# Where the decay mask and the decay powers of a fused attention and two MLPs are made, and in which order its first loads go

## The chip, the cores and the metric

The kernel runs on one core of a Trainium2 chip. The metric is the device time of one execution in microseconds (us); lower is better. One execution of the kernel before was also recorded by the hardware profiler, and every row below is from that record.

## The reference

A linear attention with a decay per head (2 batches, 8 heads, 768 positions, head dimension 64), then two MLPs over its 1,536 tokens (512 to 2048 to 512 channels), all in float32.

```python
rel = pos[:, None] - pos[None, :]
Dmask = np.where(rel >= 0, lam[:, None, None] ** rel, 0.0)
lam_pow = lam[:, None, None] ** (pos[None, :, None] + 1)
for b in range(nb):                       # blocks along the sequence
    intra = (q_b @ k_b.T * Dmask) @ v_b
    inter = (q_b * lam_pow) @ kv_state
    out_b = intra + inter
    kv_state = lam ** block * kv_state + (k_b * lam ** (block - 1 - pos)).T @ v_b
h = x @ w_in;  x = (h * tanh(softplus(h))) @ w_out
h = x @ w2_in; x = (relu(h) ** 2) @ w2_out
```

`lam` holds one number for each of the 8 heads.

## The kernel before

The sequences are cut into 12 chunks of 128 positions (6 for each batch), all heads together. A chunk c takes two loads of 512 KB, `qk{c}` (L379) and `kv{c}` (L381), and these steps, by the names that the plan gives them: `sc{c}` 16 score matmuls on TensorE (L392); `a{c}` the scores times the mask on VectorE, 128x1024; `kd{c}` keys times the last column of the mask on GpSimd (L398); `qd{c}` queries times the powers `pw` on GpSimd (L403); `sd{c}` the update of the state on TensorE (L415); `sa{c}` its addition on VectorE; `ss{c}` the decay of the state (L447 or L451); `xo{c}` the output on TensorE (L433, L437). Each result is split into a high and a low part, `xh` on ScalarE and `xl` on VectorE, since every MLP product is made of three matmuls of such parts (`mm3`, L278).

The MLP weights come as 64-bit numbers in 512 KB loads, `st{L}{g}{kind}{kk}{i}` (L502); each gives one `m` (ScalarE, L507) and one `t` (VectorE, L510), two loads together two bit operations on VectorE (L515), then `wh` (ScalarE) and `wl` (VectorE). The first MLP product, `up` of tokens 0 to 511, needs the first four weight loads (`st00000`, `st00001`, `st00010`, `st00011`) and the outputs of chunks 0 to 3. It is cut in eight groups of six matmuls; the first four need the first pair of weight loads and the first half of the channels alone.

Nothing is scheduled on the chip: the class `Plan` simulates the engines at build time, with a cost and a lag written at every `op`, and the instructions of each engine are emitted in the order that it finds. TensorE takes the ready operation of lowest rank; the other engines the one with the earliest due time. `plan.run(14.0, UNITS)` gives the time from which TensorE's work is counted when due times are worked out. The names in `FIRST` are loads (and steps of SyncE) whose order is written by hand; every other load follows the last of them. Near the end `plan.follow` holds `sc5` and `sd4` behind the third group of the first `up`. SyncE issues all large loads, one after the other; a DMA that waits there holds those behind it.

Mask and powers go through DRAM: ScalarE issues a load of `lam` onto 8 partitions; seven doubling multiplications on VectorE (`powers`, L324) make a table of 8x256 (zeros, a one, the powers); SyncE stores it to `tab_d` (L338), then reads it back with shifted addresses, 128 partitions by 4 heads by 128, in two DMAs for `mask` (L344) and two for `pw` (L351). The pieces of these four DMAs are 512 bytes each: 1,024 for the mask and 512 for the powers. TensorE starts with ten matmuls on zeros (`warm`).

Of the kernel before, what the change touches and what calls it, by code (L numbers as in the profile page):

```python
# [12 lines left out]
F32 = mybir.dt.float32  # L13
# [4 lines left out]
ALU = mybir.AluOpType  # L18
PSUM = bass.MemoryType.PSUM

P = 128
H = 8
D = 64
NP = H // 2
CH = 128
# [6 lines left out]
UNITS = 50  # L32
# [184 lines left out]
def attention_mlps(ctx, tc, lam, qk, kv, w_in, w_out, w2_in, w2_out, out):  # L217
# [7 lines left out]
    nc = tc.nc  # L225
# [9 lines left out]

    units = ctx.enter_context(tc.tile_pool(name="units", bufs=1))
    banks = ctx.enter_context(tc.tile_pool(name="banks", bufs=1, space=PSUM))
    dram = ctx.enter_context(tc.tile_pool(name="dram", bufs=1, space=bass.MemoryType.DRAM))


    FIRST = {n: 0.01 * i for i, n in enumerate(
        "st00000 qk0 tab_d kv0 st00001 masks decays qk1 kv1 qk2 kv2 qk3 kv3 st00010 st00011".split())}

    plan = Plan({"DVE": AHEAD, "ACT": AHEAD, "POOL": AHEAD, "SP": AHEAD})
    op = plan.op

    def tl(v, *shape):

        if v.tile is None:
            if v.space == "P":  # L250
                v.tile = banks.tile([P, 2, TB], F32, tag=f"b{v.slot}", name=v.name)
            else:
                v.tile = units.tile([P, 2 * TB], v.dtype, tag=f"u{v.slot}", name=v.name)
        t = v.tile
        if v.space == "P":
            if not shape:
                return t
            t = t.rearrange("p a b -> p (a b)")
        if not shape:
            shape = (2, TB)  # L260
        if len(shape) == 2:
            return t.rearrange("p (a b) -> p a b", a=shape[0])
        if len(shape) == 3:
            return t.rearrange("p (a b c) -> p a b c", a=shape[0], b=shape[1])
        return t.rearrange("p (a b c d) -> p a b c d", a=shape[0], b=shape[1], c=shape[2])
# [23 lines left out]

    W = 2 * CH
    tab_d = dram.tile([H, W], F32, name="tab_d")
    misc = Val("misc")
    mask = Val("mask")

    def pw():
        return tl(misc, 2, 4, CH)[:, 0]

    def tab():  # L300
        return tl(misc, 4, W)[0:H, 2]

    def warm_up():

# [3 lines left out]

    warm = Val("warm", "P")
    zval = Val("zero", dtype=BF16)  # L310
    misc_parts = [(misc, "pw"), (misc, "tab")]

    def zeros():
        if zval.tile is None:
# [3 lines left out]
    op("DVE", 0.4, lambda: nc.vector.memset(zeros(), 0.0), [], [(zval, 0)], name="zero", due=-9.0)  # L318
    op("PE", 4.3, warm_up, [(zval, 0)], [(warm, 0)], name="warm", rank=-3000)

    def powers():
        t, o, n = tab(), CH - 1, 1
        while n < CH:
            nc.vector.tensor_scalar(  # L324
                out=t[:, o + n + 1 : o + 2 * n + 1], in0=t[:, o + 1 : o + n + 1],
                scalar1=t[:, o + n : o + n + 1], scalar2=None, op0=ALU.mult,
            )
            n *= 2

    def ones():  # L330
        nc.vector.memset(tab()[:, 0 : CH - 1], 0.0)
        nc.vector.memset(tab()[:, CH - 1 : CH], 1.0)

    op("ACT", 0.1, lambda: nc.scalar.dma_start(out=tab()[:, CH : CH + 1], in_=lam), [], [(misc, "lam")],
       name="lam", lag=2.2, due=0.0)
    op("DVE", 0.4, ones, [], [(misc, "tab")], name="ones")
    op("DVE", 1.2, powers, [(misc, "lam")], [(misc, "tab")], name="powers")
    op("SP", 0.1, lambda: nc.sync.dma_start(out=tab_d, in_=tab()), [(misc, "tab")], [("tab_d", 0)],  # L338
       name="tab_d", lag=2.2, due=FIRST["tab_d"])

    def masks():
        for e in range(2):

            nc.sync.dma_start(  # L344
                out=tl(mask, 2, NP, CH)[:, e],
                in_=bass.AP(tab_d.tensor, tab_d.offset + e * W, [[1, P], [2 * W, NP], [1, CH]]),
            )

    def decays():
        for e in range(2):  # L350
            nc.sync.dma_start(  # L351
                out=pw()[e * D : (e + 1) * D],
                in_=bass.AP(tab_d.tensor, tab_d.offset + e * W + CH, [[0, D], [2 * W, NP], [1, CH]]),
            )

    op("SP", 1.6, masks, [("tab_d", 0)], [(mask, 0)], name="masks", due=FIRST["masks"])
    op("SP", 0.9, decays, [("tab_d", 0)], [(misc, "pw")], name="decays", due=FIRST["decays"])


    x_hi, x_lo, x_raw = {}, {}, {}  # L360
# [7 lines left out]
    def attention(j):  # L368
        cs = (2 * j, 2 * j + 1)
        t, i = divmod(j, CPB // 2)  # L370
        s, first, last = 2 * j // SEQ, 2 * j % SEQ == 0, 2 * j % SEQ == SEQ - 2
        rank = -2000 + 50 * j
        qks, kvs, avs, qds = [], [], [], []
        for c in cs:
            q, k, a = Val(f"qk{c}"), Val(f"kv{c}"), Val(f"a{c}")
# [7 lines left out]
        for n, c in enumerate(cs):  # L383
            q, k, a = qks[n], kvs[n], avs[n]
            sc = Val(f"sc{c}", "P")

            def scores(sc=sc, q=q):
                t, o = tl(q, 2, NP, CH), tl(sc, 2, NP, CH)
                for p in range(NP):
                    for e in range(2):  # L390
                        r = slice(e * D, (e + 1) * D)
                        nc.tensor.matmul(out=o[:, e, p], lhsT=t[r, 1, p], rhs=t[r, 0, p], start=True, stop=True)  # L392

            op("PE", 0.95, scores, [(q, "q"), (q, "k")], [(sc, 0)], name=sc.name, rank=rank + n)
            op("DVE", 1.3, lambda a=a, sc=sc: tt(tl(a, 2, NP, CH), tl(sc, 2, NP, CH), tl(mask, 2, NP, CH), ALU.mult),
               [(sc, 0), (mask, 0)], [(a, 0)], name=a.name)
            if not (last and n):
                op("POOL", 1.3, lambda k=k: nc.gpsimd.tensor_tensor(  # L398
                    out=tl(k, NP, 4, D)[:, :, 1:3], in0=tl(k, NP, 4, D)[:, :, 1:3],
                    in1=tl(mask, 2, NP, CH)[:, :, :, CH - 1 : CH].rearrange("p e n o -> p n e o").to_broadcast(  # L400
                        [P, NP, 2, D]), op=ALU.mult), [(k, "k"), (mask, 0)], [(k, "k")], name=f"kd{c}")
            if not first or n:
                op("POOL", 1.35, lambda q=q: nc.gpsimd.tensor_tensor(  # L403
                    out=tl(q, 2, NP, CH)[:, 0], in0=tl(q, 2, NP, CH)[:, 0], in1=pw(), op=ALU.mult),
                   [(q, "q"), (misc, "pw")], [(q, "q")], name=f"qd{c}")
        sd, xo = Val(f"sd{j}", "P"), Val(f"xo{j}", "P")
        for n, c in enumerate(cs):
            if last and n:
# [13 lines left out]
        sv = state[s]  # L422
        for n, c in enumerate(cs):
            fresh = first and n == 0

            def outs(k=kvs[n], a=avs[n], q=qks[n], n=n, fresh=fresh, sv=sv):
                v, w, qd = tl(k, NP, 4, D), tl(a, 2, NP, CH), tl(q, 2, NP, CH)[:, 0]

                z, o = tl(sv, 2, NP, P)[:, n], tl(xo, NP, 2, CH)
                for p in range(NP):  # L430
                    for e in range(2):

                        nc.tensor.matmul(out=o[e * D : (e + 1) * D, p, n], lhsT=v[:, p, 0 if e else 3],  # L433
                                         rhs=w[:, e, p], start=True, stop=fresh)
                    for e in range(0 if fresh else 2):
                        r = slice(e * D, (e + 1) * D)
                        nc.tensor.matmul(out=o[r, p, n], lhsT=z[:, p, r], rhs=qd[:, p], start=False, stop=True)  # L437

            op("PE", 0.95 if fresh else 1.9, outs,
               [(kvs[n], "v"), (avs[n], 0)] + ([] if fresh else [(qks[n], "q"), (sv, n)]),  # L440
               [(xo, n)], name=f"xo{c}", rank=rank + 20 + n)
            if last and n:
                continue
            def scale(sv=sv, n=n):
                z, last = tl(sv, 2, NP, P), pw()[:, :, CH - 1 : CH]
                if t:
                    nc.gpsimd.tensor_tensor(  # L447
                        out=z[:, 1 - n], in0=z[:, n], in1=last.to_broadcast([P, NP, P]), op=ALU.mult)
                    return
                for p in range(NP):  # L450
                    nc.scalar.activation(out=z[:, 1 - n, p], in_=z[:, n, p], func=AF.Copy, scale=last[:, p])  # L451

            if not fresh:
                op("POOL" if t else "ACT", 1.3 if t else 1.2, scale, [(sv, n), (misc, "pw")], [(sv, 1 - n)],
                   name=f"ss{c}")

            def add(sv=sv, n=n, fresh=fresh):
                z, d = tl(sv, 2, NP, P)[:, 1 - n], tl(sd, 2, 2, NP, D)[:, 0, n]
                for e in range(2):
                    r = slice(e * D, (e + 1) * D)  # L460
                    if fresh:
                        nc.vector.tensor_copy(out=z[r, :, r], in_=d[r])
                    else:
                        tt(z[r, :, r], d[r], z[r, :, r], ALU.add)

            op("DVE", 0.9, add, [(sd, n), (sv, 1 - n)], [(sv, 1 - n)], name=f"sa{c}")
# [367 lines left out]
    for o in plan.ops:  # L834
        if o.eng == "SP" and o not in ordered:
            plan.follow(ordered[-1], o)
    order = plan.run(14.0, UNITS)
    if DEBUG:
        DEBUG(plan)
    with tc.manual_schedule():  # L840
# [42 lines left out]
```

## Time and profile before

| | us |
|---|---|
| median of 3 runs | 567.02 (566.72 to 567.08) |
| span of the profiled execution, first to last instruction | 564.7 |
| TensorE matmuls busy, whole span | 549.6 (97%) |
| VectorE busy | 307.6 (54%) |
| ScalarE busy | 333.2 (59%) |
| GpSimd busy | 33.1 (6%) |

The span is 2.3 us shorter than the median; the rest lies around the first and the last instruction. The shares are means over 565 us: they say nothing of the first 35 us, in which TensorE is the least busy.

### The profile page before, as it was taken

To read this page: it belongs to the slowest core of one execution; us is meant where nothing else is said; L and a number is where in the kernel's file an instruction comes from. 1 tells how busy PE (TensorE), PEld (TensorE's weight loads), DVE (VectorE), ACT (ScalarE), POOL (GpSimd) and SP (SyncE) were. 2 spreads that over 40 slices of the span, in tenths; PEclk is the share of its full clock that TensorE was granted. 3 is DMA by queue.
4 is the path that set the end of the run, shared out by engine and by line. 5 is a ranking of instruction groups with operands and counts; after the bars stand their busy time and mean duration, and the time that the engine had idled before them with its cause. 6 is when DMAs were issued, how large, how long until landed. Compare 5 with 4: busy or idle time off the path is not lost.

```text
span 564.7 us, 7047 instructions
## 1 busy us (share of the span) xinstructions
PE 549.6 (97%) x2934; PEld 454.9 (81%) x2934; DVE 307.6 (54%) x339; ACT 333.2 (59%) x374; POOL 33.1 (6%) x31
## 2 busy tenths in 40 slices
PE   3989999999999999999999999999999999999997
PEld 1878888888888888888888888888888888888885
DVE  2876985951453833582688865434363635743301
ACT  1435364643764566545886877347964789546920
POOL 1654600000000000000000000000000000000000
PEclk9899999999999999999999999999999999999999
DMA  8999000222141106041400401311222112300022
GB/s 238 409 409 339 6 2 0 75 74 74 38 149 38 38 2 203 21 122 65 149 1 0 150 0 38 111 39 37 76 74 75 60 48 79 113 0 1 18 95 111
DMA packets 15998, 50.52 MB, mean 89 GB/s; under 512 B 1624, under 2 KB 3168, under 8 KB 15968
## 3 DMA queue, kind: packets, MB, share of 16 engines
q1 hardware_dynamic: 15952, 50.08, 25.5%
q8 instruction: 23, 0.38, 0.3%
q14 instruction: 7, 0.06, 0.0%
q10 hardware_dynamic: 16, 0.00, 0.0%
HBM read 46.92 MB, written 3.15 MB: 89 GB/s over the span
## 4 chain that ended last, share of the span: by engine, by line
PE 96%; DMA 2%; DVE 1%; issue 0%; SPq 0%; DVEq 0%
PE dn L278 46%; PE up L278 20%; PE p L278 13%; PE e L278 7%; PE b L278 3%; PE xo L433 2%; PE sc L392 2%; PE xo L437 1%; DMA mask<-tab_d 1%; PE sd L415 1%; DVE t L510 0%; DMA tab_d<-misc 0%; DVE state L271 0%; DVE misc L324 0%; DMA misc<-in_lam_dram 0%
## 5 line engine op out<-in xcount | busy, mean ns | idle before, releaser
L515 DVE SCALAR_TENSOR_TENSOR t<-m,t 128x1024 int32<-128x1024 int32 x64 | 78.5, 1231 | 63.5 <-ACT m L507 61.4
L268 ACT ACTIVATE ac<-dn 128x1024 f32<-128x1024 f32 x46 | 47.3, 1029 | 101.9 <-PE dn L278 101.9
L271 DVE TENSOR_TENSOR gl<-h,gh 128x1024 fp32r<-128x1024 f32 x48 | 58.7, 1227 | 78.0 <-ACT gh L268 77.6
L278 PE MATMUL dn<-gh,wl 128*128 128x512 f32 x192 | 74.7, 389 | 0.0
L278 PE MATMUL dn<-wh,gh 128*128 128x512 f32 x192 | 74.7, 389 | 0.0
L278 PE MATMUL dn<-wh,gl 128*128 128x512 f32 x192 | 74.7, 389 | 0.0
L278 PE MATMUL dn<-gh,wh 128*128 128x512 f32 x192 | 74.7, 389 | 0.0
L278 PE MATMUL dn<-wl,gh 128*128 128x512 f32 x192 | 74.7, 389 | 0.0
L278 PE MATMUL dn<-gl,wh 128*128 128x512 f32 x192 | 74.7, 389 | 0.0
L268 ACT ACTIVATE gh<-h 128x1024 fp32r<-128x1024 f32 x48 | 50.3, 1053 | 0.7
L507 ACT ACTIVATE m<-st 128x512 f32<-128x512 f32 x64 | 40.1, 664 | 10.5 <-DMA st<-in_moe_w_in_dram 6.8
L271 DVE TENSOR_TENSOR wl<-t,wh 128x1024 fp32r<-128x1024 f32 x32 | 39.6, 1246 | 12.1 <-ACT wh L268 12.1
L606 ACT ACTIVATE h<-up 128x1024 f32<-128x1024 f32 x20 | 20.6, 1029 | 38.2 <-PE up L278 32.5
L268 ACT ACTIVATE wh<-t 128x1024 fp32r<-128x1024 f32 x32 | 33.4, 1052 | 15.3 <-DVE t L515 15.2
L278 PEld LDWEIGHTS dn<-gh,wl 128*128 128x128 f32 x192 | 36.0, 188 | 7.5
L278 PEld LDWEIGHTS dn<-wh,gh 128*128 128x128 f32 x192 | 36.0, 188 | 7.5
L278 PEld LDWEIGHTS dn<-gl,wh 128*128 128x128 f32 x192 | 36.0, 188 | 7.5
L278 PEld LDWEIGHTS dn<-wl,gh 128*128 128x128 f32 x192 | 36.0, 188 | 7.5
L278 PEld LDWEIGHTS dn<-wh,gl 128*128 128x128 f32 x192 | 36.0, 188 | 7.4
L278 PEld LDWEIGHTS dn<-gh,wh 128*128 128x128 f32 x192 | 36.0, 188 | 7.4
L268 ACT ACTIVATE dn<-ac 128x1024 f32<-128x1024 f32 x34 | 34.4, 1019 | 0.2
L510 DVE TENSOR_SCALAR t<-st 128x512 int32<-128x512 int32 x64 | 26.8, 446 | 7.0 <-DMA st<-in_moe_w_in_dram 5.7
(102 smaller groups left out, 987.3 us busy)
## 6 DMA issues: line engine op xcount, KB each, us to landing
st<-in_moe_w_in_dram SPq DMA_DIRECT2D x32, 512.0 KB, 4.7
st<-in_moe_w_out_dram SPq DMA_DIRECT2D x32, 512.0 KB, 3.6
qk<-in_qk_dram SPq DMA_DIRECT2D x12, 512.0 KB, 10.6
kv<-in_kv_dram SPq DMA_DIRECT2D x12, 512.0 KB, 10.4
out_dram<-ac SPq DMA_DIRECT2D x4, 512.0 KB, 2.8
out_dram<-ac SPq DMA_DIRECT2D x4, 256.0 KB, 2.0
mask<-tab_d SPq DMA_DIRECT2D x2, 256.0 KB, 6.3
misc<-tab_d SPq DMA_DIRECT2D x2, 128.0 KB, 6.8
```

The costliest lines, as they stand in the source:

```text
L268: nc.scalar.activation(out=o, in_=i, func=AF.Copy)
L271: nc.vector.tensor_tensor(out=o, in0=a, in1=b, op=alu)
L278: nc.tensor.matmul(out=out_, lhsT=a, rhs=b, start=first and i == 0 and not onto, stop=last and i == 2, skip_group_check=onto)
L392: nc.tensor.matmul(out=o[:, e, p], lhsT=t[r, 1, p], rhs=t[r, 0, p], start=True, stop=True)
L415: nc.tensor.matmul(out=o[e * D : (e + 1) * D, p], lhsT=t[:, p, 1 + e], rhs=t[:, p, 0 if e else 3], start=True, stop=True)
L433: nc.tensor.matmul(out=o[e * D : (e + 1) * D, p, n], lhsT=v[:, p, 0 if e else 3], rhs=w[:, e, p], start=True, stop=fresh)
L437: nc.tensor.matmul(out=o[r, p, n], lhsT=z[:, p, r], rhs=qd[:, p], start=False, stop=True)
L507: op("ACT", 0.67, lambda st=st, i=i: nc.scalar.activation(out=tl(m)[:, i], in_=tl(st, TB, 2)[:, :, 1].bitcast(F32), func=AF.Copy, scale=RA ...
L510: op("DVE", 0.5, lambda st=st, i=i: nc.vector.tensor_scalar(out=tl(t)[:, i], in0=tl(st, TB, 2)[:, :, 0], scalar1=29, scalar2=None, op0=ALU ...
L515: nc.vector.scalar_tensor_tensor(out=tl(t), in0=tl(m).bitcast(I32), scalar=scalar, in1=tl(t), op0=shift, op1=ALU.bitwise_or)
L606: op("ACT", 1.05, lambda: nc.scalar.activation(out=tl(h), in_=tl(src), func=AF.Relu if L else AF.Mish), halves(src), [(h, 0)], name=h.name)
```

## The change

The table in DRAM goes away with its store and its four reads. ScalarE loads `lam` repeated on all 128 partitions (`rate`, 8 values each), and twice more, onto 64 partitions each, every second value of it (`pair_rate`, 4 values). GpSimd writes a 128x128 diagonal of ones. VectorE makes each head's mask as one scan along 128 columns: `state = lam * state + eye`, which is 0 left of the diagonal, 1 on it, then the powers. Eight such scans make the mask (two operations of four, `mask0` and `mask1`), four scans with a start of 1 and nothing added make `pw`. SyncE now issues `qk0 kv0 qk1 kv1` first, then the first two weight loads, then chunks 2 and 3 and the next two weight loads as before. The due times are worked out from 6.0 instead of 14.0.

```diff
     FIRST = {n: 0.01 * i for i, n in enumerate(
-        "st00000 qk0 tab_d kv0 st00001 masks decays qk1 kv1 qk2 kv2 qk3 kv3 st00010 st00011".split())}
+        "qk0 kv0 qk1 kv1 st00000 st00001 qk2 kv2 qk3 kv3 st00010 st00011".split())}
...
-    op("ACT", 0.1, lambda: nc.scalar.dma_start(out=tab()[:, CH : CH + 1], in_=lam), [], [(misc, "lam")],
-       name="lam", lag=2.2, due=0.0)
-    op("DVE", 0.4, ones, [], [(misc, "tab")], name="ones")
-    op("DVE", 1.2, powers, [(misc, "lam")], [(misc, "tab")], name="powers")
-    op("SP", 0.1, lambda: nc.sync.dma_start(out=tab_d, in_=tab()), [(misc, "tab")], [("tab_d", 0)],
-       name="tab_d", lag=2.2, due=FIRST["tab_d"])
...
+    def diagonal():
+        nc.gpsimd.memset(tl(misc, 2, 4, CH)[:, 1, 0:2], 0.0)
+        nc.gpsimd.affine_select(out=eye(), in_=eye(), pattern=[[1, CH]], compare_op=ALU.not_equal, fill=1.0,
+                                base=1 - CH, channel_multiplier=1)
+
+    def rates():
+        nc.scalar.dma_start(out=rate(), in_=bass.AP(lam.tensor, lam.offset, [[0, P], [1, H]]))
         for e in range(2):
...
+            nc.scalar.dma_start(out=pair_rate()[e * D : (e + 1) * D],
+                                in_=bass.AP(lam.tensor, lam.offset + e, [[0, D], [2, NP]]))
+
+    op("ACT", 0.3, rates, [], [(misc, "lam")], name="lam", lag=2.2, due=-9.0)
+    op("POOL", 0.9, diagonal, [], [(misc, "eye")], name="eye", due=-9.0)
+
+    def run_of_powers(out_, lam_, add, first):
+        nc.vector.tensor_tensor_scan(out=out_, data0=lam_.to_broadcast([P, CH]), data1=add, initial=first,
+                                     op0=ALU.mult, op1=ALU.add)
+
+    def masks(n):
+        for h in range(4 * n, 4 * n + 4):
+            run_of_powers(tl(mask, 2, NP, CH)[:, h % 2, h // 2], rate()[:, h : h + 1], eye(), 0.0)
...
     def decays():
...
-    op("SP", 1.6, masks, [("tab_d", 0)], [(mask, 0)], name="masks", due=FIRST["masks"])
-    op("SP", 0.9, decays, [("tab_d", 0)], [(misc, "pw")], name="decays", due=FIRST["decays"])
+        for p in range(NP):
+            run_of_powers(pw()[:, p], pair_rate()[:, p : p + 1], none(), 1.0)
+
+    for n in range(2):
+        op("DVE", 1.3, lambda n=n: masks(n), [(misc, "lam"), (misc, "eye")], [(mask, n)], name=f"mask{n}", due=-8.0 + n)
+    op("DVE", 1.3, decays, [(misc, "lam"), (misc, "eye")], [(misc, "pw")], name="decay", due=2.0)
...
-    order = plan.run(14.0, UNITS)
+    order = plan.run(6.0, UNITS)
```

## Rows read from the trace of the kernel before

**Rows 1.** TensorE's waits, whole span: who waited for whom, us in total, times, longest.
```profile
PE xo L433 <- DVE a L271: 6.8, 1, 6.8
PE sc L392 <- DMA qk<-in_qk_dram: 2.6, 2, 1.3
```

**Rows 2.** Four stretches: length, busy us by engine, granted clock, DMA share, GB/s.
```profile
0.00:13.03 13.03, 5.12 (x26) 2.26 (x26) 2.81 (x13) 2.62 (x3) 1.16 (x5) 0.94 0.84 236
...
14.31:18.84 4.53, 4.53 (x48) 3.91 (x49) 2.80 (x3) 1.06 (x1) 2.21 (x3) 0.57 1.03 410
18.84:32.45 13.61, 11.67 (x213) 10.62 (x209) 12.69 (x18) 7.16 (x18) 7.84 (x7) 1.00 1.03 409
32.45:560.90 528.45, 528.18 (x2652) 438.11 (x2652) 287.36 (x306) 322.39 (x352) 20.62 (x16) 1.00 0.22 75
```

**Rows 3.** The chain that ended last, first 20 us: start, us, what.
```profile
0.73 1.38 DMA misc<-in_lam_dram
...
3.92 1.78 DMA tab_d<-misc
...
6.15 6.75 DMA mask<-tab_d
...
13.03 1.23 DVE a L271
...
16.28 2.01 PE sc L392 x16
...
18.91 1.09 PE sc L392 x16
```

**Rows 4.** Instructions in order of time, first 8 us: start, us, engine, line, operation.
```profile
0.73 0.58 ACTq L334 DMA_DIRECT2D misc<-in_lam_dram  x1
...
1.19 3.96 PE L307 MATMUL warm<-zero 128*128 128x512 bf16 x10 [1.19 <-DVE zero L318]
...
5.11 0.67 ACT L507 ACTIVATE m<-st 128x512 f32<-128x512 f32 x1 [2.48 <-DMA st<-in_moe_w_in_dram]
...
5.11 0.43 DVE L510 TENSOR_SCALAR t<-st 128x512 int32<-128x512 int32 x1 [1.22 <-DMA st<-in_moe_w_in_dram]
...
6.37 1.16 PE L392 MATMUL sc<-qk 64*128 64x128 f32 x16 [1.22 <-DMA qk<-in_qk_dram]
6.70 1.43 SPq L351 DMA_DIRECT2D misc<-tab_d  x2
```

**Rows 5.** Busy time and DMA in one stretch of 1 us, columns as in Rows 2.
```profile
8.00:9.00 1.00, 0.00 (x0) 0.00 (x0) 0.00 (x0) 0.00 (x0) 0.00 (x0) 1.00 1.01 195
```

**Rows 6.** VectorE's groups from 12.9 to 32.5 us: count, busy us, mean ns, idle before.
```profile
L271 DVE TENSOR_TENSOR a<-sc,mask 128x1024 f32<-128x1024 f32 x4 | 4.9, 1222 | 4.3 <-DMA mask<-tab_d 2.5 <-PE sc L392 1.7
L515 DVE SCALAR_TENSOR_TENSOR t<-m,t 128x1024 int32<-128x1024 int32 x3 | 3.7, 1222 | 0.1
L271 DVE TENSOR_TENSOR state<-sd,state 64x256 f32<-64x256 f32 x6 | 2.5, 422 | 0.6 <-PE sd L415 0.4
L510 DVE TENSOR_SCALAR t<-st 128x512 int32<-128x512 int32 x2 | 2.3, 1202 | 0.0
L271 DVE TENSOR_TENSOR xl<-xo,xh 128x512 fp32r<-128x512 f32 x3 | 2.1, 688 | 0.1
L271 DVE TENSOR_TENSOR wl<-t,wh 128x1024 fp32r<-128x1024 f32 x1 | 1.4, 1369 | 0.0
L462 DVE COPY state<-sd 64x256 f32<-64x256 f32 x2 | 0.8, 416 | 0.0
```

**Rows 7.** Instructions in order of time where the first up begins.
```profile
31.13 1.16 PE L392 MATMUL sc<-qk 64*128 64x128 f32 x16 [1.33 <-DMA qk<-in_qk_dram]
...
32.45 0.47 PE L278 MATMUL up<-xh,wh 128*128 128x512 f32 x1 [0.16 <-DVE state L271]
```

**Rows 8.** VectorE, in order of time: a late input of the second token block's up.
```profile
63.65 1.23 DVE L271 TENSOR_TENSOR fl<-xr,fh 128x1024 fp32r<-128x1024 f32 x1
```

**Rows 9.** The chain that ended last: start, us, what, for that up's first matmuls.
```profile
66.34 2.95 PE up L278 x12
```

More of the change, by code (lines that the diff above doesn't have):

```diff
@@ L237, in attention_mlps @@
     banks = ctx.enter_context(tc.tile_pool(name="banks", bufs=1, space=PSUM))
-    dram = ctx.enter_context(tc.tile_pool(name="dram", bufs=1, space=bass.MemoryType.DRAM))
     FIRST = {n: 0.01 * i for i, n in enumerate(
-        "st00000 qk0 tab_d kv0 st00001 masks decays qk1 kv1 qk2 kv2 qk3 kv3 st00010 st00011".split())}
+        "qk0 kv0 qk1 kv1 st00000 st00001 qk2 kv2 qk3 kv3 st00010 st00011".split())}
     plan = Plan({"DVE": AHEAD, "ACT": AHEAD, "POOL": AHEAD, "SP": AHEAD})
@@ L288, in halves @@
         return [(v, 0), (v, 1)]
-    W = 2 * CH
-    tab_d = dram.tile([H, W], F32, name="tab_d")
     misc = Val("misc")
@@ L298, in pw, with eye, none, rate @@
         return tl(misc, 2, 4, CH)[:, 0]
-    def tab():
-        return tl(misc, 4, W)[0:H, 2]
+    def eye():
+        return tl(misc, 8, CH)[:, 4]
+    def none():
+        return tl(misc, 8, CH)[:, 5]
+    def rate():
+        return tl(misc, 8, CH)[:, 6, 0:H]
+    def pair_rate():
+        return tl(misc, 8, CH)[:, 7, 0:NP]
     def warm_up():
@@ L310, in attention_mlps @@
     zval = Val("zero", dtype=BF16)
-    misc_parts = [(misc, "pw"), (misc, "tab")]
     def zeros():
@@ L319, in attention_mlps @@
     op("PE", 4.3, warm_up, [(zval, 0)], [(warm, 0)], name="warm", rank=-3000)
[L321 to L332, printed above, removed]
@@ L334, in attention_mlps @@
-    op("ACT", 0.1, lambda: nc.scalar.dma_start(out=tab()[:, CH : CH + 1], in_=lam), [], [(misc, "lam")],
-       name="lam", lag=2.2, due=0.0)
-    op("DVE", 0.4, ones, [], [(misc, "tab")], name="ones")
-    op("DVE", 1.2, powers, [(misc, "lam")], [(misc, "tab")], name="powers")
-    op("SP", 0.1, lambda: nc.sync.dma_start(out=tab_d, in_=tab()), [(misc, "tab")], [("tab_d", 0)],
-       name="tab_d", lag=2.2, due=FIRST["tab_d"])
-    def masks():
-        for e in range(2):
[L344 to L347, printed above, removed]
@@ L349, in decays @@
-    def decays():
[L350 to L354, printed above, removed]
-    op("SP", 1.6, masks, [("tab_d", 0)], [(mask, 0)], name="masks", due=FIRST["masks"])
-    op("SP", 0.9, decays, [("tab_d", 0)], [(misc, "pw")], name="decays", due=FIRST["decays"])
+    def diagonal():
+        nc.gpsimd.memset(tl(misc, 2, 4, CH)[:, 1, 0:2], 0.0)
+        nc.gpsimd.affine_select(out=eye(), in_=eye(), pattern=[[1, CH]], compare_op=ALU.not_equal, fill=1.0,
+                                base=1 - CH, channel_multiplier=1)
@@ L360, in attention_mlps @@
+    masked = [(mask, 0), (mask, 1)]
+    decayed = [(misc, "pw")]
     x_hi, x_lo, x_raw = {}, {}, {}
@@ L395, in attention @@
             op("DVE", 1.3, lambda a=a, sc=sc: tt(tl(a, 2, NP, CH), tl(sc, 2, NP, CH), tl(mask, 2, NP, CH), ALU.mult),
-               [(sc, 0), (mask, 0)], [(a, 0)], name=a.name)
+               [(sc, 0), *masked], [(a, 0)], name=a.name)
             if not (last and n):
@@ L400, in attention @@
                     in1=tl(mask, 2, NP, CH)[:, :, :, CH - 1 : CH].rearrange("p e n o -> p n e o").to_broadcast(
-                        [P, NP, 2, D]), op=ALU.mult), [(k, "k"), (mask, 0)], [(k, "k")], name=f"kd{c}")
+                        [P, NP, 2, D]), op=ALU.mult), [(k, "k"), *masked], [(k, "k")], name=f"kd{c}")
             if not first or n:
@@ L404, in attention @@
                     out=tl(q, 2, NP, CH)[:, 0], in0=tl(q, 2, NP, CH)[:, 0], in1=pw(), op=ALU.mult),
-                   [(q, "q"), (misc, "pw")], [(q, "q")], name=f"qd{c}")
+                   [(q, "q"), *decayed], [(q, "q")], name=f"qd{c}")
         sd, xo = Val(f"sd{j}", "P"), Val(f"xo{j}", "P")
@@ L453, in attention @@
             if not fresh:
-                op("POOL" if t else "ACT", 1.3 if t else 1.2, scale, [(sv, n), (misc, "pw")], [(sv, 1 - n)],
+                op("POOL" if t else "ACT", 1.3 if t else 1.2, scale, [(sv, n), *decayed], [(sv, 1 - n)],
                    name=f"ss{c}")
```

## The prediction

> **What bounds the kernel now.** I read the stretches first [rows 2]. From 32.45 us on, TensorE is busy 528.18 of 528.45 us: no other engine and no DMA can give back more than 0.27 us there. Whatever the change is worth is therefore decided before the first `up` product, and the question is only how much earlier TensorE can reach that point with the same work done. The waits of TensorE [rows 1] say where it loses time: one wait of 6.8 us of the first `xo` for the first masked scores, and 2.6 us in two waits of score matmuls for `qk` loads. The chain [rows 3] tells what stands behind the long one: `lam` lands at 2.11, the table is stored by 5.70, the mask lands at 12.90 and the first `a` begins at 13.03. After the pause TensorE's clock is also low: in 14.31 to 18.84 the granted clock is 0.57 of full, a mixture of the levels 1.2 and 2.4 GHz [rows 2], after an idle stretch that began when the first scores ended at 7.5 [rows 4]. The same 16 score matmuls take 2.01 us there and 1.09 later [rows 3].
>
> The last thing to see is that three resources are close together between 13 and 32 us. DMA moves 409 to 410 GB/s with a share of 1.03 [rows 2], so it is full; VectorE is busy 12.69 of 13.61 us and TensorE 11.67. The removal of the mask's wait is therefore not worth what the wait was; it is worth the smallest of three leads.
>
> **The change part by part.**
>
> *Removed.* The table's path: from the landing of `lam` at 2.11 to the first `a` at 13.03 [rows 3]. SyncE loses five DMA issues, two of which take 1.43 us together [rows 4], and the wait for the table that held `kv0` and everything behind it. 1,536 pieces of 512 bytes leave the DMA queues. In 8 to 9 us the DMA engines are full at 195 GB/s [rows 5] against 409, which is at most 381 such pieces in a microsecond.
>
> *Added, ScalarE.* Three DMA issues in place of one, 0.58 us each by the one there is [rows 4], so until about 2.5. ScalarE's next useful work waits for a weight load that will land after 10, so the issue time is hidden; if it weren't, it would cost 1.2 us. The loads have 128 pieces of 32 bytes and 512 of 4 bytes. At the rate of the small pieces above, 640 pieces are 1.7 us of all DMA engines; zero if they slip between the large ones. I take 0.5 us off the large loads. `rate` should land like `lam`, at 2.1 to 3.4; the last `pair_rate` at 3.4 (issued at about 2.0, plus 1.38) to some 6.
>
> The Trainium skill (DMA: Bandwidth & Descriptors, Queues, rings and completion order) says that each DMA engine takes turns between the queues that have work, so ScalarE's small loads would not have to wait behind all of SyncE's large ones. The landing of `lam` at 2.11 with a 512 KB load already issued agrees but tests it little, as that load had hardly begun to move.
>
> *Added, GpSimd.* A memset of 256 columns and a select of 128, before anything else that matters; its memset of 1024 columns of state moves behind them. No row shows a select; GpSimd has nothing to do until the mask is there, so I count nothing, and 1 us if the diagonal comes after `rate`.
>
> *Added, VectorE.* Twelve scans of 128 elements. No row shows a scan. Two-source operations take 422 ns for 256 and 1222 for 1024 elements [rows 6], that is 1.04 ns an element and 0.155 fixed, so 0.29 us for 128 as a lower end. Each step of a scan needs the one before it, so it may go slower for each element; I take the row of twice the length, 0.42, and 0.9, about twice that again, as the upper end, since no row excludes it. Twelve are 5.0 us (3.5 to 10.8): from about 2.4, masks are ready at 5.8, powers at 7.5, and the first `a` begins at some 7.7. The powers stand ahead of `a` since the plan finds them ready first.
>
> The Trainium skill (DVE: opcode table, instruction layouts, handler registers and perf-mode slots, Datapath and trigger behaviour) says that the built-in scan runs at half throughput. By that a scan of 128 would cost what 256 elements cost otherwise, an estimate that equals the row I chose; without it the twelve would be 3.5 us and `a` 1.5 us earlier. No run here shows it yet.
>
> *Moved.* `qk0 kv0 qk1 kv1` before the weights, and no table in between. The first load landed at 5.1, the second at 6.37 [rows 4]; a load is 0.524 MB, or 1.28 us at 409 GB/s. So load n lands at 5.1 + 1.28 (n - 1), plus the 0.5: `qk1` near 8, the two weight loads near 11 and 12, `kv3` near 17, the next weights by 19.7, the 17th load at 26.1. The first scores follow the warm-up, which ends at 5.15 [rows 4], about 1.2 earlier than before.
>
> *The sum: when can `up` begin?*
> - TensorE: the work between is 1.16 + 4.53 + 11.67 = 17.4 us [rows 2, 4], less 1.9 if the clock stays at 2.4 GHz (0.92 on the scores, as much again on the `xo` before them). From 5.15 that is 20.6 at the earliest.
> - VectorE: the groups of 12.9 to 32.5 sum to 17.7 us [rows 6], plus 0.9 for two `t` of the first weights, 0.43 each [rows 4], that used to fall into the pause. From 7.7: 26.3 without any idle time. 3.5 us of it (two `t` of 1.2 each and the third bit operation) belong to weights that only the second half of `up` reads: 22.8 if the new order puts them later. With 1 to 2 us of waiting for loads: 24 to 27.5.
> - DMA: six score blocks stand before `up`, and `sc5` is held behind its third group, so the sixth is `sc6`, which waits for the 17th load [rows 7]. If the plan keeps that order, `up` begins at 26.1 + 1.1 = 27.2, 5.2 us earlier than 32.45. If `up` goes first, it begins with VectorE at about 25.5, and `sc6`'s 1.1 us comes later: 32.45 - 25.5 - 1.1 = 5.9.
>
> Both orders give much the same, and I take 5.6 us. The wait of 6.8 and the slow clock's 1.9 would have given 8.7; the difference goes to loads and to VectorE. Of the rest of the span I take the 0.27 of idle time and the 3.8 us after the last matmul as they are. Span 564.7 - 5.6 = 559.1; with the 2.3 us around it 561.4.
>
> **The rivals.**
>
> *A (less gain): the small loads or the scans hold the first `a`.* For it: 512 four-byte pieces on a queue beside full loads, and no row of a scan. Each microsecond that the powers come later moves VectorE's 26.3 by as much. With the powers' `lam` at 6 and 0.6 us a scan, `a` begins near 9.7 and the lead is 2 to 4: 563 to 565. Against it: VectorE can put off 3.5 us.
>
> *B (more gain): the order puts the second weights off.* `up` begins at about 23 with the clock high all along, lead 7 to 8.5, 558.5 to 560. Against it: loads land only at their rate, and the planned order had those operations ahead before.
>
> *C (no change): the lead is given back later.* All orders after 32.45 are planned anew, with due times 8 us earlier. The last `fl` for `up` of the next tokens ends at 64.88 and its matmuls begin at 66.34 [rows 8, 9]: 1.5 us to spare. If VectorE, with 5 us of scans more, comes there no earlier than now, TensorE waits until then and keeps 1.5 at most: 565.5 to 567. Against it: its inputs come earlier too, and over the whole stretch it is busy 287.36 of 528.45 us [rows 2], though that row doesn't say how much of the idle time lies before 65.
>
> *D (slower): scans beyond 0.9 us.* `a` begins later than 13.03 as soon as twelve scans take more than 13.03 - 2.4 = 10.6 us, 0.89 each. At 1.2 us each it is 16.8, 3.8 us later than now, and VectorE's other work is stacked behind, while the earlier `qk` loads can't help: about 570. For it: nothing shows a scan, and a broadcast operand. Against it: of VectorE's groups with 512 or fewer elements [rows 6] only the two `t` take that long, the others 0.69 or less.
>
> **How the numbers follow.** Forecast (lead 4.2 to 7): 0.60, 560 to 562.8. A 0.16, B 0.11, C 0.07, D 0.06. The range reaches into A and B: 558.6 to 564.6. About 0.2% (1.1 us) is what a measurement of this kernel can tell from no change. Faster by more: forecast, A and B, 0.87; within it: most of C, 0.07; slower: D, 0.06.
>
> **What would show it.** `a` first at 7 to 9; scans at 0.3 to 0.5 us; no wait of `xo` above 3 us, and a granted clock near 1.0 from 9 us on; `up` first at 24 to 27.5; DMA at about 410 GB/s from 4 us on; idle time of TensorE after `up` under 1 us. The prediction is wrong if scans or small loads are far from these, or if TensorE gets a new wait between 33 and 80 us.

## The result, and the profile after

The changed kernel takes 569.16 us (median of 5 runs, 568.97 to 571.12), the kernel before 566.72 beside it (566.05 to 567.08): a ratio of 1.0051, 95% interval 1.0034 to 1.0069. It is slower by half a per cent, where 561.4 us was forecast. The profiled execution, 571.12, is the slowest of the five; its span is 569.3 us. Its rows show where the time lies; of how much, the medians (2.4 us) say more than the spans (4.6).

TensorE's waits in the changed kernel: who waited for whom, us in total, times, longest [rows 1].

```profile
PE xo L432 <- DVE a L270: 4.5, 2, 3.6
PE sc L391 <- DMA qk<-in_qk_dram: 3.6, 1, 3.6
PE up L277 <- DVE xl L270: 1.7, 1, 1.7
```

The wait of `xo` for the first masked scores was to shrink from 6.8 us to under 3. It is 3.6 at its longest, but a wait of 3.6 for `qk1` stands beside it, and a new one of 1.7 at the first `up`. The chain that ended last says what is behind it: start, us, what [rows 3].

```profile
1.92 12.53 DMA misc<-in_lam_dram
...
14.88 1.03 DVE misc L341 x3
15.91 1.13 DVE a L270
...
17.08 1.98 PE xo L432 x16
...
36.02 9.15 PE up L277 x32
```

A load of 1 KB, the second `pair_rate`, was issued by 1.92 and landed at 14.45. The first `a` begins at 15.83 (the chain enters it at 15.91), 2.8 us later than before, and `up`, which starts at 33.60 and then waits for `xl`, runs without a wait only from 36.02, 3.6 later than before. All three small loads were slow. Loads by what they fill: engine, count, size, median us from issue to landing.

```profile
misc<-in_lam_dram ACTq DMA_DIRECT2D x2, 1.0 KB, 10.4
misc<-in_lam_dram ACTq DMA_DIRECT2D x1, 4.0 KB, 4.9
```

And while they were under way the large loads were slow. Stretches of the changed kernel, columns as in [rows 2]; the last three figures are the granted clock, the share of the 16 DMA engines and GB/s.

```profile
5.00:6.00 1.00, 1.00 (x9) 0.44 (x8) 0.27 (x1) 0.00 (x0) 0.00 (x0) 1.00 0.79 312
6.00:7.00 1.00, 0.72 (x14) 0.53 (x10) 1.00 (x4) 0.00 (x0) 0.00 (x0) 1.00 0.16 41
7.00:8.00 1.00, 0.00 (x0) 0.00 (x0) 1.00 (x5) 0.00 (x0) 0.00 (x0) 1.00 0.38 131
...
11.00:12.00 1.00, 1.00 (x14) 1.00 (x12) 0.00 (x0) 0.00 (x0) 0.00 (x0) 0.50 0.56 156
...
5.60:17.08 11.48, 4.25 (x49) 3.65 (x48) 5.17 (x14) 0.66 (x1) 3.15 (x3) 0.65 0.74 277
17.08:23.50 6.42, 6.17 (x66) 5.52 (x66) 3.83 (x8) 1.85 (x5) 1.29 (x2) 0.57 1.03 416
...
36.02:46.02 10.00, 10.00 (x42) 7.90 (x44) 5.98 (x5) 2.70 (x3) 4.21 (x4) 0.83 1.02 409
...
36.02:565.50 529.48, 529.21 (x2650) 439.08 (x2650) 286.19 (x305) 321.94 (x352) 19.29 (x15) 1.00 0.21 71
```

In the microsecond from 6 the DMA engines are busy for a sixth of their time and move 41 GB/s; from 11 it is 156 GB/s with a share of 0.56. They are not full, although large loads are waiting: by 6 us six have been issued, and the 1.0 MB that has moved is less than two of them. `qk1` comes late, TensorE idles from 6.7 to 10.3, and the granted clock falls from 1.00 to 0.50, the 1.2 GHz level. It stays low until the first outputs are done (0.65 and 0.57 in the two stretches) and dips once more after the wait at `up` (0.83 from 36 us on).

The span is therefore longer by 36.02 - 32.45 = 3.57 us ahead of `up`, and by 529.48 - 528.45 = 1.03 after it, which is the low clock: TensorE's idle time there is 0.27 us, as in [rows 2]. (A clock of 0.83 over ten microseconds is 1.7 us of full speed, an estimate; 0.6 of it doesn't show, since the first two matmuls of `up` had run at 33.60.) Together 4.6.

SyncE, which issues only large loads, stood still too: its own waits, and its issues in order of time.

```profile
SPq L378 <- DMA misc<-in_lam_dram: 4.7, 1, 4.7
...
SPq L501 <- DMA misc<-in_lam_dram: 2.2, 1, 2.2
```

```profile
2.67 3.31 SPq L501 DMA_DIRECT2D st<-in_moe_w_in_dram  x2
...
9.38 0.33 SPq L380 DMA_DIRECT2D kv<-in_kv_dram  x1
14.46 0.33 SPq L378 DMA_DIRECT2D qk<-in_qk_dram  x1
```

Two weight issues that take 0.9 us together from 15.31 on take 3.31 here, 2.2 of it a wait for a load of `lam`, and between two further issues lie 5 us that end with the landing of the last one, although no large load reads `lam`. This wait is not what slows the loads: by 14.46 eight large loads had been issued, and the 3.0 MB moved by then are less than six of them, so there was always a load to move.

What the change was meant to do, it does: the scans are short and the diagonal is hidden. VectorE, in order of time.

```profile
5.73 2.63 DVE L341 TENSOR_TENSOR_SCAN mask<-misc 128x128 f32<-128x128 f32 x8 [4.60 <-DMA misc<-in_lam_dram]
14.54 1.37 DVE L341 TENSOR_TENSOR_SCAN misc<-misc 128x128 f32<-128x128 f32 x4 [6.18 <-DMA misc<-in_lam_dram]
```

Eight scans have their results by 8.36; the four of the powers wait another 6.18 us for their factors.

### The profile page after: what moved, and what is told of

It is laid out like the page before. It is cut to its first block, busy times and chain, and to the rows that moved or that the text cites. A ratio compares the mean times of both kernels' runs of the same rounds, so it can differ in the third digit from the quotient of the medians.

```text
span 569.3 us, 7051 instructions
## 1 busy us (share of the span) xinstructions
PE 553.9 (97%) x2934; PEld 458.2 (80%) x2934; DVE 308.2 (54%) x342; ACT 332.6 (58%) x374; POOL 36.3 (6%) x33
## 4 chain that ended last, share of the span: by engine, by line
PE 94%; DMA 2%; DVE 2%; issue 1%; ACTq 0%; DVEq 0%
PE dn L277 46%; PE up L277 20%; PE p L277 13%; PE e L277 7%; PE b L277 3%; DMA misc<-in_lam_dram 2%; PE xo L432 2%; PE xo L436 1%; PE sc L391 1%; PE sd L414 1%; DVE a L270 1%; DVE xl L270 0%; DVE state L270 0%; DVE wl L270 0%; DVE misc L341 0%
## 5 line engine op out<-in xcount | busy, mean ns | idle before, releaser
L277 PE MATMUL up<-xl,wh 128*128 128x512 f32 x64 | 25.6, 400 | 1.7 <-DVE xl L270 1.7
## 6 DMA issues: line engine op xcount, KB each, us to landing
qk<-in_qk_dram SPq DMA_DIRECT2D x12, 512.0 KB, 10.4
kv<-in_kv_dram SPq DMA_DIRECT2D x12, 512.0 KB, 10.4
misc<-in_lam_dram ACTq DMA_DIRECT2D x2, 1.0 KB, 10.4
```

The costliest lines, as they stand in the source:

```text
L277: nc.tensor.matmul(out=out_, lhsT=a, rhs=b, start=first and i == 0 and not onto, stop=last and i == 2, skip_group_check=onto)
```

## The experiments

The theory, P ('pieces' in the expectations): the 512 pieces of 4 bytes of the two `pair_rate` loads cost several microseconds by themselves, and they take them from every load that is under way. Its rivals: L, it is only that the powers come late and `a` stands behind them; O ('order'), it is the new order of the loads or of the plan; S ('scans'), the scans. Two expectations add 'turns': a piece is cheap, and slow only where it stands beside large loads. Every kernel is compared with the kernel before, run beside it; the ratio is to that, with its 95% interval. The expectations call the kernels by the labels in brackets.

**The pieces alone** (e2_before_with_pieces). In the kernel before, the two loads are added and nobody reads them:

```diff
+        for e in range(2):
+            nc.scalar.dma_start(out=tl(misc, 8, CH)[e * D : (e + 1) * D, 7, 0:NP],
+                                in_=bass.AP(lam.tensor, lam.offset + e, [[0, D], [2, NP]]))
```

> The kernel before with the two loads of pair_rate added behind its own lam load, into columns that nobody reads. Theory 'pieces': even unread they slow SyncE's loads and the four DMAs of the table in the first 14 us; the mask lands 3 to 8 us later than 12.9, and the kernel is 2 to 6 us slower: 569 to 573. Rivals 'order' and 'scans': unread loads cost nothing, 566.5 to 567.2.

568.79 us, ratio 1.0044 (1.0030 to 1.0058): 2.2 us for two loads of 1 KB that nothing waits for by name, the low end of what was expected; the first `a` begins at 14.85, 1.8 us later, less than expected. The store of the table, 1.78 us before [rows 3], now takes 6.15 to land, and SyncE waits for it. Its wait, then two stretches meanwhile, then the packets of 6 to 9 us (queue and kind: packets, MB, share of the 16 engines):

```profile
SPq L349 <- DMA tab_d<-misc: 4.9, 1, 4.9
```

```profile
6.00:7.00 1.00, 0.89 (x16) 0.90 (x16) 0.00 (x0) 0.00 (x0) 0.00 (x0) 1.00 0.05 0
7.00:8.00 1.00, 0.27 (x6) 0.08 (x2) 0.00 (x0) 0.00 (x0) 0.00 (x0) 1.00 0.04 0
```

```profile
q10 hardware_dynamic: 289, 0.00, 4.3%
```

In 3 us, 289 pieces pass and next to nothing else, about 10 ns a piece, with the engines busy 4% of the time. SyncE's `kv0` and `st00001`, issued behind the store at 4.33 and 4.73, move nothing from 6 to 8 us.

**Without the pieces** (e1_pairs_on_chip). The two loads go; GpSimd copies the values out of `rate`:

```diff
-        for e in range(2):
-            nc.scalar.dma_start(out=pair_rate()[e * D : (e + 1) * D],
-                                in_=bass.AP(lam.tensor, lam.offset + e, [[0, D], [2, NP]]))
+    def pairs():
+        for e in range(2):
+            r = slice(e * D, (e + 1) * D)
+            nc.gpsimd.tensor_copy(out=pair_rate()[r], in_=rate()[r].rearrange("p (n e) -> p n e", e=2)[:, :, e])
```

> The changed kernel without its two loads of pair_rate: GpSimd copies the 4 values of each half from rate, which already holds all 8 on every partition (two copies of 64x4). Theory 'pieces' (the 512 pieces of 4 bytes hold the powers until 14.5 and starve the large loads between 2 and 14 us): the scans of the powers follow those of the mask at once, before 9 us; DMA is near 400 GB/s from 5 us on; the first up begins near 26 to 27.5 instead of 33.6; 561 to 563. Rival 'order' (the new order of loads and due times brings the first weights and VectorE's chain late): powers early, but up still after 31 and 566 or more. Rival 'scans' (VectorE's twelve scans are the cost): they are still there, so 567 or more.

565.28 us, 0.9979 (0.9964 to 0.9995): 3.9 better than the changed kernel, and faster than before by 0.2%. The twelve scans are still there, so S falls. The 561 to 563 that P expected is missed: the first `a` is at 11.76, `up` runs from 30.96, and DMA moves 410 GB/s from 6 us on; but `rate`, 128 pieces of 32 bytes, lands only at 6.2. VectorE and TensorE, in order of time:

```profile
11.76 2.32 DVE L270 TENSOR_TENSOR a<-sc,mask 128x1024 f32<-128x1024 f32 x2
...
30.96 0.50 PE L277 MATMUL up<-xl,wh 128*128 128x512 f32 x1 [1.27 <-DVE xl L270]
```

**Is it the late landing or the slowed loads?** (e11_unread_pieces) The kernel just shown, with the two loads put back and unread, as in the first experiment:

> As e1_pairs_on_chip (powers from copies of rate), with the two pair_rate loads kept, into columns that nobody reads. It parts the two harms of the 512 pieces. If it is the slowing of the large loads: as the changed kernel, 568 to 569.5. If it is the late landing of the powers' lam that VectorE waits for: as e1_pairs_on_chip, 565 to 566. Expected is the first, since qk1 landed at 10.3 in the changed kernel against 8.8 in e1_pairs_on_chip and the following loads later still.

568.95 us, 1.0036 (1.0018 to 1.0054), the time of the changed kernel within the intervals. The powers are ready at 10.4 here, 5.5 us earlier than there, and it gains nothing that can be told from noise: L falls. What is as in the changed kernel are the loads. The ten runs lie from 566.67 to 570.58 us, the four slowest with the lowest mean granted clock (0.988), so the 3.7 us above the kernel without the pieces is the middle of a wide spread. TensorE's and SyncE's waits, and two stretches:

```profile
PE sc L398 <- DMA qk<-in_qk_dram: 7.5, 4, 3.6
```

```profile
SPq L385 <- DMA misc<-in_lam_dram: 4.3, 1, 4.3
```

```profile
6.00:7.00 1.00, 0.73 (x14) 0.53 (x10) 1.00 (x5) 0.00 (x0) 0.94 (x2) 1.00 0.15 41
...
11.00:12.00 1.00, 1.00 (x12) 1.00 (x12) 0.48 (x1) 0.00 (x0) 0.00 (x0) 0.50 0.52 164
```

**Half the pieces** (e8_one_pair_load). One of the two loads stays (`range(1)`), the other half is copied on GpSimd:

> The changed kernel with one of its two pair_rate loads (256 pieces of 4 bytes); the other half is copied from rate by GpSimd. VectorE's order is that of the changed kernel. If the cost grows with the number of pieces: the load lands near 10 instead of 14.5, and the time lies between e1_pairs_on_chip and the changed kernel, 566 to 568. If one such load does all the harm: 568.5 or more.

566.58 us, 1.0001 (0.9982 to 1.0020). With 0, 256 and 512 pieces the time is 565.3, 566.6 and 569.2, so the cost seems to grow with the number. The runs of this kernel lie from 565.24 to 569.08: the step from 256 to 512 is clear of the intervals, the one from 0 to 256 is not.

**All of `lam` on SyncE's queue** (e5_lam_on_sync_queue), ahead of `qk0`, so that the large loads are queued behind the pieces rather than beside them:

```diff
-        nc.scalar.dma_start(out=rate(), in_=bass.AP(lam.tensor, lam.offset, [[0, P], [1, H]]))
+        nc.sync.dma_start(out=rate(), in_=bass.AP(lam.tensor, lam.offset, [[0, P], [1, H]]))
...
-            nc.scalar.dma_start(out=pair_rate()[e * D : (e + 1) * D],
+            nc.sync.dma_start(out=pair_rate()[e * D : (e + 1) * D],
```

> The changed kernel with all three lam loads (128 pieces of 32 bytes, 512 of 4) issued by SyncE ahead of qk0, so they share one queue with the large loads and none runs beside them. Theory 'turns' (a small piece is cheap, about 110 in a microsecond when no large load moves, but on a queue of its own each piece waits its turn behind pieces of 4 KB, and the large loads are slowed in return): the powers' lam lands by 5 to 7 us instead of 14.5, the large loads start about 2 to 4 us later than in the kernel before but run at 400 GB/s; 563 to 566. Theory 'pieces' (the time is that of the pieces, wherever they are issued): lands at 10 or later, 568 or more.

569.11 us, 1.0046 (1.0030 to 1.0062): the time on ScalarE's queue again, as P expected. It shows the pieces by themselves. Stretches, and the packets from 2 to 7 us:

```profile
3.00:4.00 1.00, 1.00 (x4) 0.32 (x3) 0.64 (x2) 0.00 (x0) 0.19 (x1) 1.00 0.04 0
...
6.00:7.00 1.00, 0.00 (x0) 0.00 (x0) 0.00 (x0) 0.00 (x0) 0.00 (x0) 1.00 0.03 0
7.00:8.00 1.00, 0.00 (x0) 0.00 (x0) 0.00 (x0) 0.00 (x0) 0.00 (x0) 1.00 0.19 45
```

```profile
q1 hardware_dynamic: 487, 0.00, 4.4%
```

487 pieces in 5 us (some of them `rate`'s of 32 bytes), again about 10 ns each, in engines that are busy 4.4% of the time; the large loads behind them begin in the eighth microsecond. By this pace the 512 pieces are 5.3 us (an estimate from this row and the one of 6 to 9 us above). On a queue of their own they overlap some of the large loads and slow the rest. The two totals are the same, but the price is not: the kernels without the 512 pieces take 565.28 us with `rate` on ScalarE's queue and 563.15 with it on SyncE's (next), so they cost 3.9 us there and 6.0 here.

**`rate` alone on SyncE's queue** (e6_rate_on_sync_queue), ahead of `qk0`, the pairs copied on GpSimd as before:

> As e1_pairs_on_chip (no pair_rate loads), with the one load of rate issued by SyncE ahead of qk0 instead of by ScalarE beside it. Theory 'turns': rate lands at 2.3 to 3 us instead of 6.2, large loads run at 400 GB/s from 4 us on instead of 150 until 5; first a at 8 to 9 instead of 11.8; 561.5 to 564. Theory 'pieces': 128 pieces cost the same on either queue, rate lands at 5 or later, within 0.7 us of e1_pairs_on_chip (565.3).

563.15 us, 0.9936 (0.9920 to 0.9953), the fastest of all and faster than both kernels, as 'turns' expected: 128 pieces of 32 bytes cost 2.1 us less ahead of the large loads than beside them. `rate` lands at 3.64, the first `a` begins at 8.34, the clock is 1.00 up to 13 us, and DMA moves 422 GB/s from 4 us on, but for a dip to 229 from 9 to 10. The chain that ended last:

```profile
1.16 4.13 DMA qk<-in_qk_dram
...
5.32 12.20 DMA qk<-in_qk_dram
...
17.54 10.21 DMA qk<-in_qk_dram
...
27.89 1.16 PE sc L395 x16
29.05 8.44 PE up L277 x36
```

Nothing of `lam` is left in it: it runs over `qk` loads, as the forecast's DMA bound said. `up` begins 32.45 - 29.05 = 3.4 us earlier than before, and the medians differ by 3.5.

**The order of loads and the plan's start** (e3_loads_weights_first, e4_start_14, e7_rate_on_sync_weights_first). The kernel without the pieces with `st00000 qk0 kv0 st00001 qk1 kv1` as the first loads; the kernel without the pieces, its order left, with `plan.run(14.0, UNITS)`; and the fastest with the first of these orders:

> As e1_pairs_on_chip, but the first loads in the order that the kernel before has: st00000, qk0, kv0, st00001, qk1, kv1. Theory 'pieces': the order of six loads is worth 1.3 us a place at the most, so within 1.5 us of e1_pairs_on_chip. Rival 'order': 3 us or more faster than e1_pairs_on_chip.

> As e1_pairs_on_chip, but due times worked out from 14.0 as in the kernel before. Theory 'pieces': due times only arrange work among VectorE, ScalarE, GpSimd and SyncE, so within 1 us of e1_pairs_on_chip. Rival 'order': 2 us or more faster than e1_pairs_on_chip, with another order on VectorE before up.

> As e6_rate_on_sync_queue, with the first loads in the order of the kernel before (st00000 qk0 kv0 st00001 qk1 kv1). e3_loads_weights_first was 0.7 us faster than e1_pairs_on_chip. If what bounds the way to up is VectorE's chain through the first weights, again 0.5 to 1.5 us faster than e6_rate_on_sync_queue; if it is the chunk loads, slower by about as much.

564.6 (0.9965, 0.9954 to 0.9976) and 565.35 (0.9986, 0.9974 to 0.9997) against 565.28; 563.4 (0.9947, 0.9927 to 0.9967) against 563.15. Of all three the intervals overlap those of the kernels they vary. O falls: the order is worth 0.7 us at most, in no single direction (neither way that the third expectation named is seen).

**Is the last `qk` the bound?** (e9_sc6_after_up) In the fastest kernel `sc6` too is held behind the third group of `up`:

```diff
-    for n in ("sc5", "sd4"):
+    for n in ("sc5", "sd4", "sc6"):
         plan.follow(named["up000100"], named[n])
```

> As e6_rate_on_sync_queue, but sc6 is held behind the third group of up as sc5 and sd4 are, so that the 17th load no longer stands before up. In e6_rate_on_sync_queue every step of the chain before up is a landing of qk, the last at 27.75, and up begins at 29.05. Theory 'loads bound the start' : up begins at 26 to 28, and since sc6's 1.1 us comes later the gain is small, 0.3 to 1.5 us (561.7 to 562.9). Rival 'VectorE bounds it': up waits for xl until 29 or later and the time stays within 0.4 us of 563.15 or grows.

565.58 us, 0.9969 (0.9955 to 0.9982): 2.4 slower, where a gain was expected. `up` starts at 26.26 and then stands still for `xl` until 29.32. TensorE's waits, then VectorE in order of time:

```profile
PE up L277 <- DVE xl L270: 2.3, 1, 2.3
```

```profile
23.97 2.59 DVE L513 TENSOR_SCALAR t<-st 128x512 int32<-128x512 int32 x2
26.59 1.95 DVE L518 SCALAR_TENSOR_TENSOR t<-m,t 128x1024 int32<-128x1024 int32 x1
28.57 0.69 DVE L270 TENSOR_TENSOR xl<-xo,xh 128x512 fp32r<-128x512 f32 x1
```

VectorE reaches that `xl` at 28.57, hardly earlier than in the fastest kernel (28.76), so two bounds lie on top of each other, the loads and VectorE. That is why nothing is gained; what is lost is in the main `sc6`'s 1.1 us behind `up`, and the clock. The ten microseconds after the wait here, and those from the start of `up` in the fastest kernel:

```profile
29.32:39.32 10.00, 10.00 (x42) 7.89 (x44) 4.04 (x4) 2.69 (x3) 5.27 (x4) 0.83 1.03 410
```

```profile
29.05:39.05 10.00, 10.00 (x68) 8.04 (x68) 6.90 (x7) 3.79 (x4) 4.70 (x5) 1.00 1.03 410
```

A clock of 0.83 instead of 1.00 is 1.7 us of full speed (an estimate from the first row). And 4.5 us of what stands ahead of this `xl` is work on the second pair of weights, which only the second half of `up` reads.

**`lam` as one piece** (e10_lam_spread_by_tensor, e12_spread_before_warm). Based on the kernel without the pieces: one load of 32 bytes onto one partition, spread over the others by a product with ones on TensorE, copied to `rate` by VectorE. In the first kernel the product was to follow three of the ten warm-up products, but the plan put it behind all ten; in the second one more line holds it between the third and the fourth:

```diff
+    op("ACT", 0.3, lambda: nc.scalar.dma_start(out=tl(row)[0:1, 0, 0:H], in_=bass.AP(lam.tensor, lam.offset, [[0, 1], [1, H]])),
+       [], [(row, 0)], name="lam", lag=2.2, due=-9.0)
...
+    op("PE", 0.1, lambda: nc.tensor.matmul(out=tl(warm)[:, 1, 0:H], lhsT=tl(row)[0:1, 1, 0:P], rhs=tl(row)[0:1, 0, 0:H],
+                                           start=True, stop=True), [(row, 0), (row, 1)], [(warm, 1)], name="spread", rank=-3001)
...
+    op("DVE", 0.2, lambda: nc.vector.tensor_copy(out=rate(), in_=tl(warm)[:, 1, 0:H]), [(warm, 1)], [(misc, "lam")],
+       name="rate", due=-8.8)
```

```diff
+    plan.follow(named["spread"], named["warm"])
```

> As e6_rate_on_sync_queue, but lam comes as one piece of 32 bytes on one partition and a matmul with a row of ones spreads it over the partitions (after three of the ten warm-up matmuls); VectorE copies the 8 columns out. No small pieces are left. If the 128 pieces of rate still cost the large loads time in e6_rate_on_sync_queue (52 GB/s from 2 to 3 us, 230 from 3 to 4): qk loads land 0.5 to 1.2 us earlier and the time is 562 to 562.8. If 128 pieces ahead of the loads cost nothing that counts: within 0.4 us of 563.15.

> lam is loaded as one 32 B piece on one partition and spread by a matmul, as in e10, but the matmul now stands ahead of seven of the ten warm-up groups, so that rate should be there near 3 us instead of 5.41. If the landing of lam is what sets the end, the first scans start near 3.1 us, the first a comes near 8 us and the time is 562 to 563.5 us, as in e6. If it is VectorE's work before the first up, stretched beside GpSimd in the order that the plan gives it, up waits for xl again and the time stays at 565 or more.

570.01 us (1.0063, 1.0048 to 1.0078) and 570.13 (1.0048, 1.0029 to 1.0068), both slower than before; neither expectation of the first came true. The second (its runs lie from 566.73 to 570.94) is over 565 as its rival had it, but doesn't settle what it was made for: the product moved to 2.58, but VectorE's copy still waited for the last warm-up. Its row, then the first kernel's GpSimd and VectorE side by side:

```profile
6.26 0.17 DVE L339 COPY misc<-warm 128x8 f32<-128x8 f32 x1 [5.00 <-PE warm L313]
```

```profile
14.89 1.06 POOL L407 TENSOR_TENSOR kv<-kv,mask 128x512 f32<-128x512 f32 x1 [2.23 <-DMA kv<-in_kv_dram]
14.94 2.71 DVE L519 TENSOR_SCALAR t<-st 128x512 int32<-128x512 int32 x2
...
15.90 1.46 POOL L412 TENSOR_TENSOR qk<-qk,misc 128x512 f32<-128x512 f32 x1
...
18.52 1.27 POOL L412 TENSOR_TENSOR qk<-qk,misc 128x512 f32<-128x512 f32 x1
18.56 2.31 DVE L524 SCALAR_TENSOR_TENSOR t<-m,t 128x1024 int32<-128x1024 int32 x1
```

In the first one the first `a` begins at 11.18, near the 11.76 of the kernel that it is based on, but `up` runs only from 35.12 instead of 30.96. Beside GpSimd's products a `t` takes 1.36 us, which takes 0.43 alone [rows 4], and a bit operation 2.31 instead of 1.22 [rows 6]. In the kernel it is based on, the same two `t` take 1.41 together and the bit operation 1.23, so these rows are 2.4 of the 4.2 us; the rest, and the second kernel's 4.3 us wait for `xl`, stay open. In the ten microseconds from 35 the granted clock is 0.83 in the first kernel and 0.74 in the second, where the kernel that they are based on has 1.00 from 30.96 on.

## Why the prediction was wrong, step by step

*The step that failed* is the price of ScalarE's small loads: "At the rate of the small pieces above, 640 pieces are 1.7 us of all DMA engines; zero if they slip between the large ones. I take 0.5 us off the large loads." The rate came from a row in which the engines were full [rows 5], and even that row holds few small pieces, 38 of its 82 packets:

```profile
DMA packets 82, 0.19 MB, mean 195 GB/s; under 512 B 10, under 2 KB 38, under 8 KB 82
```

The engines are not what limits 4-byte pieces: 487 pieces used 4.4% of the engines and took 5 us all the same. What the 512 cost this kernel is 3.9 us (changed kernel against the one without them; 3.7 with them unread), and 2.2 in the kernel before. `rate`'s 128 pieces beside the loads cost another 2.1, so ScalarE's small loads, put at 0.5 us, cost 6.0 against a single such load ahead of the large ones (569.16 against 563.15). They are most of the 7.8 us between forecast and result; the 1.8 that are left are the second term below. The last load, put at 3.4 "to some 6", landed at 14.45. `rate`, put at 2.1 to 3.4, landed at 5.7 beside large loads and at 3.64 ahead of them.

The Trainium skill (DMA: Bandwidth & Descriptors, Queues, rings and completion order) has the DMA engines take turns between queues with work. No run here shows such turns: from 6 to 8 us of the first experiment `kv0` and `st00001` are issued and move nothing while the pieces of the other queue pass, and whether their own pieces had reached the engines by then can't be seen. `rate` did gain by going ahead, 2.8 us to land instead of 4.9 to 5.5. The large loads were not spared on either queue: the 512 pieces cost 3.9 us on ScalarE's and 6.0 on SyncE's.

*A second term was too small.* Without the pieces, with `rate` early and DMA full from 4 us but for one dip, the forecast's own premises nearly hold, and the lead is 3.5 us, not 5.6. The loads: the 17th landed at 27.75, not 26.1. VectorE: I had `up` 16.3 to 19.8 us behind the first `a` (24 to 27.5 from 7.7). It ran without a break 20.2 us behind it in the changed kernel, 19.2 without the pieces, 20.7 in the fastest, against 19.4 before. The "22.8 if the new order puts them later" never came: in the changed and the fastest kernel the second weights stayed ahead of `xl`. And GpSimd now works beside VectorE: the four powers' scans took 2.19 us instead of 1.37 in the fastest kernel, and 1.35 in the one with the other order of loads, where GpSimd did nothing from 6 to 8 us.

*The clock.* "Near 1.0 from 9 us on" was 0.50 from 9 us: the idle stretch moved from before `xo` to before `qk1`'s scores, 6.7 to 10.3, and the clock fell there. In the fastest kernel it is 1.00 up to 13 us and 0.89 from there to `up`.

*What was right.* The scans: 0.40 us each beside 0.42 taken, so rival D falls. The Trainium skill's half throughput for the built-in scan (DVE: opcode table, instruction layouts, handler registers and perf-mode slots, Datapath and trigger behaviour) agrees: 398 ns for 128 elements is nearly what 256 cost otherwise [rows 6]. The diagonal: 0.31 and 0.29 us on GpSimd, done by 1.4. Nothing is given back later (rival C): idle time after `up` is 0.27 us as before. And the reading that all is decided before the first `up`: 3.57 of the 4.6 us lie there.

*The rivals.* A named the cause, small loads beside full ones, but let the harm pass through the powers and stopped at 565. The unread pieces show the other way: the large loads starve, TensorE idles, the clock falls. In the changed kernel both ways end close together, so its chain runs through the powers; taking the powers off it gained nothing.

*What stays open.* Why a piece takes 10 ns when the engines are idle: these runs don't tell the making of the pieces from their passage. Why SyncE's issues stop until `lam`'s pieces have landed isn't shown either, but it is no property of `lam`: in the fastest kernel's chain, too, `qk` issues start at 5.32 and 17.54, each 0.03 us or less behind the landing of an earlier `qk` (5.29 and 17.52). Nor is it known why DMA falls to 229 GB/s from 9 to 10 us in the fastest kernel; the same kernel with the other order of loads has 418 there and takes the same time.

## What to carry to other kernels

Price a DMA by the number of its separate pieces as well as by its bytes: 512 pieces of 4 bytes, 2 KB in all, took back more here than the whole path through DRAM with its 1,536 pieces of 512 bytes had cost. Load such values in whole rows, ahead of the large loads, and rearrange them on an engine that is idle. When several resources end within a microsecond or two of each other, a wait that goes away is worth only the distance to the next, so work it out for each of them before believing the sum.

## What the runs showed of the hardware

Small pieces, most of them of 4 bytes, pass at about 100 in a microsecond where nothing large moves (487 in 5 us, 289 in 3 us), on either queue and with the 16 engines 4% busy, and while they pass, loads of the other queue stall: the table's store took 6.15 us to land instead of 1.78, and loads already issued moved 0 GB/s from 6 to 8 us. A load of 128 pieces of 32 bytes took 4.9 to 5.5 us beside large loads and 2.8 ahead of them. VectorE's shorter operations stretch beside GpSimd's products: a `t` from 0.43 to 1.36 us, the powers' four scans from 1.37 to 2.98 in the kernel without the pieces.
